# Transposing two chunks of P on TensorE: threshold attention with a maxout FFN on one Trainium2 core

## The chip, the cores and the metric

The kernel runs on one core of one Trainium2 chip (trn2). The metric is the device time of one execution in microseconds (us); lower is better. A core has five engines that run side by side, each with its own instructions in order: TensorE (PE, matmul; its weight loads are shown as PEld), VectorE (DVE), ScalarE (ACT), GpSimd (POOL) and SyncE (SP), which issues transfers here. PE writes into PSUM; DVE and ACT read it from there.

## The reference

Inputs are q, k, v of shape (8, 8, 576, 64) (batch, heads, rows, head size), a scalar tau of 0.02, three FFN weights w1, w2, w3 of (512, 768) and w_out of (768, 512). All are float32.

```python
scores = scale * np.matmul(q, k.transpose(0, 1, 3, 2))        # scale = 1/8
thresh = np.max(scores, axis=-1, keepdims=True) - tau
scores = np.where(scores >= thresh, scores, -1000000000.0)
scores = scores - np.max(scores, axis=-1, keepdims=True)
attn = np.exp(scores)
attn = attn / (np.sum(attn, axis=-1, keepdims=True) + 1e-09)
attn_out = np.matmul(attn, v)
x = attn_out.transpose(0, 2, 1, 3).reshape(B * S, H * D)      # 4608 x 512
h = np.maximum(np.maximum(x @ w1, x @ w2), x @ w3)
out = h @ w_out
```

## The kernel before

**Tiling.** The heads are taken in 16 groups of four (two groups to a batch). A group's scores are computed in nine chunks of 128 rows, each in two halves of 128 x 576, so there are 144 chunks and 288 halves. The variable `n` of a chunk is its place in this count, from 0. After both groups of a batch have their attention products, the batch's FFN runs: 18 hidden pieces (6 column blocks by 3 weights) and output pieces.

**An order written out by hand.** All engines are fed from one string, `ORDER`. Each letter issues one step, and the digit behind S, T, O and F names which of four PSUM slots (two banks each) it uses. `line` holds, for each letter, the queue of items whose earlier step has been issued. The engines run their own steps in the order of the string, and each step waits for its data and its buffers. What moves in the string moves on the engine. The letters that matter here:

- S: a half's score matmuls on PE (`scores`); T: PE transposes of q or k; O: a product of P and v on PE (`product`); F and B: the first and second half of an FFN piece on PE.
- m: DVE reads a score half and takes its maximum (`maximum`). e: ACT's first pass (`exponents`). n: ACT's second pass, or k: DVE's product with a mask (`numerators`).
- r: DVE's reciprocal of the sums. p: POOL scales one half into `P` in bf16 (`normalized`); a chunk takes two.
- t: SP issues a DMA transpose of `P` into `ptq` (`turned`). ptq is what the products read, one for each group.
- l, g, o: SP's loads of q, k, v, its loads of weights, its stores. y, z: POOL's casts of v and of weights; q: POOL's swapped copy of q.
- a, c: ACT's and DVE's copies of transposed q and k out of PSUM. x, w: ACT's and DVE's copies of a product. h, v: ACT's copy of a first FFN piece, and DVE's maximum. u: ACT's copy of an output piece.

**Masks.** `MASKED` has one digit for each of the 288 halves. With 1 the half is masked by DVE: m writes `z` into SBUF and so frees the PSUM slot, e is one ACT pass on that, and k is a DVE pass. With 0, m only reads, e reads PSUM and frees the slot, and n is a second ACT pass. So a 1 moves work from ACT to DVE.

**Buffers.** P has 6 buffers (`PBUFS`), `z` has 4 for each of the two halves (`ZBUFS`), ptq has 2.

Every step is recorded by a helper at one line, L90, so the profile names that line for nearly all of them; they are told apart by the tile names (sc scores, tp transposes of q and k, o products, ph hidden pieces, po output pieces, ptq transposed P).

Of the kernel before, what the change touches and what calls it, by code (L numbers as in the profile page):

```python
# [12 lines left out]
BF16 = mybir.dt.bfloat16  # L13
# [25 lines left out]
ORDER = """
lllS0llmlS1yelgS2ymylS3emgnlT0mleS1lakS2nlqermS3ylmeS0pmeS1kpS3elmS2nlzmelrmnT1pS0tcnperkT1pameS1zmteS3knpS0  # L40
rnmpemS2permeqS1mnqT3meqktepS0ncS2ntrpmS3npretprmeS1pmnS0tpmS3npmS1etpmeS0rT2mnplkeT1akgeS2qmgepmteS3rkpeknt
S0perrnmT2pncS3ptamepS1meqtrS2meyqnS3lmqeS0pmelpknT1lpS2nmeymeS3lrkepS0tcnT2rpnmS1tpnmaprrmS0eS2pmteS1pmT3ep
ctepmeT3O0ykntnyS2etrykpnO1wnprmaS0xptrS3meS2zmeS1mzgeS0mlnS3pmleS1pmelO2qmelpkteO0nrnklpS3nlwgxprrmS2leS0pm
eF3qtmT1eBqcF0eqkthBpnS2vS1nF3pmnF0pmBerBkepS2vhT1tnprmS0S3apmetS1zmeS2rmpeF3tmF0epBkepF1tnBvBznvS2ghS3rymnF
0gmS1eplBrkepF2tnmF3BnpvBnqvT1S0hprrcT2S3pamS1eymzF2emBeqgkF0etyS3nS1vpnmtF2pBmezBveS3prgnS0mtS1phrmT3epO2me
tzeF0wpnS1gcqS2nmBqnmO3zekepgS1xvlF2nS3mtnF0rrmpBeBlpveS1lphS2mntF3zmeBrpS0evS1lpnmF2lnpS3rmleBptmS1nzvS0nS3
mtpnS2rpeF1rmepmtepS0mBepmtekF3ektekT2uBarklpukS0uqlS2urS1mlnS3pmleO0pmlepmelO2wtnkS1xrS0tepmF2myF3eBkepT1tB
hcF0nqvT2T1laByrcynS3qvS2nlqmF1tnpF0meS3pBelmBlhrrF2kpelS1vnBlprF3mnlS0pveBtprmS1hS2pmeS3tpmeS0pmF2emF1eBkeT
3BvatF0nvqT2T3BkqlaS1nrcS3phmtS2npmF0epF1mteBqkBeqF3lnvS2lnBrvplS0hmtpS1F3meS2mteBrmepS0vnpO1rekpnO3mtnpweS2
yrrtxS1mF0yymT3epBcnS1pvS2nptF3meS0pmeBomT2hS1okeF0omF3ntBkaBervS1ponrF2vpemS0ptuS3mpeF2metknT1T3rknBparrceS  # L50
0puS3mqtuS1mpeS2mpeS3lmF0peomepS1ketqT3S2ncBqnmlqnmlO3ekluktO1urnwperrS0pxS3mptnS2mS1pempS3etmF0peF2meBlkBel
S1khoF3nrmlF0pnBtvpBerrvS2phlS1mnpS3tmF0peS2mpeBmeF3vF1eoBkntS0vnBS2rmhpS3mepS1mteyF2mF0eyBkteBnrvT3pF1aovT2
ynBplrcS3hplS0mnyF2lmF1elBykepBlnvT3tS0aS2vnO3rrmtpnmpeS1weptS2mS0prmO3eqtmeqF1eqlT0S2xqcBnlpmS3hlpS0meF2ymF
1elBknlF3vnBokBetS2hvS0nrrF3mpF1mpeBkBpetF2vnprS0uvnT3ptmS2aS1pmeS0trmF3epmnpkeS2tS0ermpBnmopnkS1uS2rurompS0
eF3ompelmpeS2lkpeS0lmS1elqBmelqmetkO2unktO0erwpurkpT1txT2cS3apF0nmtT1qS2ceBqmnS1yF3hmF2eyrBpeBvptnF0pS1vnBrm
tpS3hS2pmeS0mtS1eF3meF2meBkBeF0knF1vnBBrvhpS3nvT0pF2akyF1tnBmyS0velByrmlS3phS2rlempF1lmyeF0pklBepS3tnvS2nBrm
ptO1meprvepS2wnS3plmF0nF1rmepBlkeqS2lBhmtT3nyS0vnS2mqlO1emtpecT2xT0rS3pacF1eqmF2lnyBklqeT0BvlaS3khoS1qnmF0tF
2pmeBrBopnvS3teprvF0pnrmS1puS2meS3prmS0epF1tmepmepT2ktBeqncT3tuS0kaS2urqmS3tnpmS1nF0pmemteS3repS1mS2lepmBely
kteS3kuO1rumplnmlpO0ewterpT2xS1cqnoS3mpF0nF2metBkeBkF1hlF3nvBlnrrS0pvlnBpmS2lhS1ymleF0mtS3epBmepF2vF1etkBnS0
vnS3rmBnpS2rhmpF0emF1pteBkpBerF3vnS2ptvnT0pBramS1pthS0mepF3meqtT2rBecpS1nvylT0ynS2pmlS3amlS1eomS0elO2rmpeome  # L60
plO3ketnwT1F0nctF2xkBnBrvpS1hrF3pmS0qBemqS2onvF1yeF0mBopkeF3tyBnS2vqhBrlrnmpT1S0vaptS2empF1S3mpelBkeplF0vntS
2rumS1pnS0mtepF3rmepmetqS2kS0epBnmmteS1rkepS2lmuS0ulpmS1nlymT3yetF2cekeT3oBrknpamoS0npS3mnS1qtmuO0qurrmqelO2
wpelkpelS0xS3meptF2mS1peBemytF0hrkT3pBecF2nS1vpnS3rymtBpnmS0epS1vlnF3mF2etBmeBkhF0lkeF3nBrvpS1nrvBpnS2mptS0h
mpeS3meF2tmF1eBkeBlrvnT0plS3ravlpS2nlmqF0nlS1mqeBtrrmpF2eS3phBlmepS0tvepS1mS2npS3mepO0meknO1meownT3orxkT2pS0
tacF1nF2qrmeBtpS3evpBmS0tyhF1meT2yBcqoeF3rpkT2F0aptBnvBnS2pvS1hqtmF3nqT0meBrS1npvF2npmT3BactS1ervF3prmS0pueS
2ompF3ekqelmT1ntS0qcnBpmekteS2S1urrmpF0uompekS3eptS2nmS1pnmlO3ermtpekO2pnwS1ykxtyS3emS2BomeyrmepS1rukpS2uoF3
meF0opmnBtykBhpS1ervS2eptmO3pO0mxnS3txS2rmepF0empF1ekBtBevF3hkS2nS0mnBrmF1npF2vepBkBtS0hvO3emO2xkS1xerS3rpmF
2mpF0eF1kpteBnBvpF3BvtBrhkpF2S0vS1prmBptmF3eF0pveBtBhS1vS2mS3mF0F1mBkBF2vhF3keBeO0vnO1kF2kxeBwurS1rvpS0mpS2F
3mpetmpeS0eoF1mnketBknkBurrupoF2puF0hptF3uvF2pvF1hF0tvF3rvpF2hF1vopF0vF3thF2vF1vF0hoF3vF2ovF1hF0vF3vO2uoO1wF
0xF3F2hF1vF3vF2hF1vF3vF2hF1vF3vF2hF1vF3vF2hF1vF3vF2hF1vBvF3uuooBF2uuuooo  # L70
"""


# [28 lines left out]
def kernel(  # L102
# [485 lines left out]
    def flow(what, fn):  # L588
        while True:
# [13 lines left out]
    def issue(what, where):  # L603
        if what == "S":
            c, r = next(todo["S"])
            c[r] = scores(Ls[c["g"]], c["idx"], r, where)
            line["m"].append((c, r))
        elif what == "T":
            g, n, r = next(todo["T"])
            p = transposed(Ls[g], n, r)  # L610
            p.first(where)
            line["a" if n == "q" else "c"].append((p, g, r))
        elif what == "O":
            p = next(todo["O"])
            p.first(where)
            for k, fn in (("x", p.scalar), ("w", p.vector)):
                if fn:
                    line[k].append(fn)
        elif what == "F":
            p = next(todo["F"])  # L620
            p.first(where)
            if p.second:
                pending.append(p)
            else:
                line[p.kind].extend(p.done)
        elif what == "B":
            p = pending.pop(0)
            p.second()
            line[p.kind].extend(p.done)
        elif what == "m":  # L630
            c, r = line["m"].pop(0)
            c["bias", r] = maximum(c, r)
            line["e"].append((c, r))
        elif what == "e":
            c, r = line["e"].pop(0)
            exponents(c, r)
            line["k" if masked(c["g"], c["idx"], r) else "n"].append((c, r))
        elif what in "nk":
# [36 lines left out]
_INS = ['q', 'k', 'v', 'tau', 'moe_w1', 'moe_w2', 'moe_w3', 'moe_w_out']  # L675
# [31 lines left out]
```

## Time and profile before

| what | before |
|---|---|
| time, median of 3 runs | 446.44 us (446.01 to 447.31) |
| profiled execution, its own time | 447.21 us |
| its span from first to last instruction | 445.4 us |
| mean granted TensorE clock | 0.985 |
| busy PE, DVE, ACT, POOL | 425.5, 395.1, 393.8, 314.9 us |
| P transposes by DMA | 144, median 3.9 us from issue to landing |
| first product of P and v starts | 54.9 us |
| first FFN piece starts | 67.8 us |

Times within the execution are counted from the start of the span. An engine's busy time counts its instructions' spans; spans of neighbouring instructions on an engine overlap, so the start-to-start time is shorter than a duration. The page's slices cut the span into 40 parts of about 11 us, with the busy share in tenths.

### The profile page before, as it was taken

What the parts mean: (1) busy time and instruction counts of PE and PEld (TensorE: products, weight loads), DVE (VectorE), ACT (ScalarE), POOL (GpSimd) and SP (SyncE); (2) the same over time, 40 slices, a digit from 0 to 9 for tenths busy, and PEclk for the clock granted to TensorE, in tenths of its full rate; (3) what the DMA queues carried; (4) which work ended last, traced back from release to release, by engine and by line L of the source; (5) the groups of instructions that cost most, each with busy time, mean ns of one, the idle gap of its engine ahead of it and who ended that gap; (6) DMA issues with size and microseconds to landing.
All of it is one profiled execution on the core that took longest, in us unless ns stands there. A gap on an engine that the chain in (4) does not pass through costs nothing.

```text
span 445.4 us, 14085 instructions
## 1 busy us (share of the span) xinstructions
PE 425.5 (96%) x5195; PEld 316.4 (71%) x5195; DVE 395.1 (89%) x1093; ACT 393.8 (88%) x801; POOL 314.9 (71%) x417
## 2 busy tenths in 40 slices
PE   7677799999999999999999999999999999999995
PEld 5455557767787767778687767867687778777772
DVE  4889999999999999989989998999999999989641
ACT  4999999999999999999998999999999999956422
POOL 3797999989686686686768884859767789562300
PEclk9967999999999999999999999999999999999999
DMA  7999999999999988999996999899998978872902
GB/s 235 344 163 216 251 169 241 227 245 230 222 250 195 244 165 177 252 191 253 187 175 158 238 206 167 207 249 203 208 208 192 249 121 172 149 122 34 217 13 107
DMA packets 212773, 87.44 MB, mean 196 GB/s; under 512 B 185824, under 2 KB 199648, under 8 KB 212704
## 3 DMA queue, kind: packets, MB, share of 16 engines
q1 hardware_dynamic: 212000, 85.69, 92.2%
q8 instruction: 41, 0.67, 0.6%
q10 hardware_dynamic: 704, 0.85, 0.6%
q14 instruction: 28, 0.23, 0.2%
HBM read 34.60 MB, written 9.44 MB: 99 GB/s over the span
## 4 chain that ended last, share of the span: by engine, by line
PE 82%; DVE 6%; ACT 5%; issue 3%; DMA 2%; POOL 1%; SPq 1%; DVEq 0%; POOLq 0%; ACTq 0%
PE ph L90 30%; PE sc L90 28%; PE po L90 11%; PE o L90 9%; ACT z L90 4%; PE tp L90 4%; DVE unused L90 2%; DVE z L90 2%; DMA km<-in_k_dram 1%; DMA qm<-in_q_dram 1%; POOL P L90 1%; SPq L90 1%; DVE hm L90 0%; DVE hT L90 0%; DVE kt L90 0%
## 5 line engine op out<-in xcount | busy, mean ns | idle before, releaser
L90 POOL TENSOR_SCALAR P<-z,rs 128x576 bf16<-128x576 f32 x288 | 229.5, 812 | 85.1 <-DVE rs L90 36.8
L90 PE MATMUL sc<-kt,qs 64*128 64x256 f32 (+2 forms) x640 | 180.5, 423 | 4.8 <-DVE z L90 1.7
L90 PE MATMUL sc<-kt,qt 64*128 64x320 f32 (+2 forms) x640 | 181.1, 434 | 4.1 <-ACT z L90 4.1
L90 PE MATMUL ph<-xt,w 64*128 64x288 bf16 (+2 forms) x2160 | 163.8, 283 | 0.3
L90 PEld LDWEIGHTS <-w 64*128 64x128 bf16 (+1 forms) x2160 | 124.8, 94 | 31.0 <-issue 5.1
L90 DVE TENSOR_SCALAR_CACHE_REDUCE unused<-sc 128x576 bf16<-128x576 f32 x183 | 133.3, 750 | 8.5 <-PE sc L90 7.5
L90 ACT ACTIVATE z<-sc,nm 128x576 f32<-128x576 f32 x183 | 131.2, 740 | 10.5 <-DVE unused L90 6.8
L90 ACT ACTIVATE z<-z 128x576 f32<-128x576 f32 x183 | 123.5, 681 | 0.1
L90 PEld LDWEIGHTS sc<-kt,qs 64*128 64x128 f32 (+1 forms) x640 | 94.3, 181 | 25.5 <-ACT z L90 7.0
L90 PEld LDWEIGHTS sc<-kt,qt 64*128 64x128 f32 (+1 forms) x640 | 94.5, 181 | 17.8 <-ACT z L90 9.2
L90 DVE SCALAR_TENSOR_TENSOR z<-z 128x576 f32<-128x576 f32 x105 | 85.2, 822 | 0.8 <-ACT z L90 0.8
L90 DVE TENSOR_SCALAR_CACHE_REDUCE z<-sc 128x576 f32<-128x576 f32 x105 | 77.7, 752 | 5.8 <-PE sc L90 3.5
L90 ACT ACTIVATE z<-z,nm 128x576 f32<-128x576 f32 x105 | 79.0, 773 | 3.5 <-DVE z L90 3.2
L90 POOL COPY qs<-qt 64x512 f32<-64x512 f32 (+1 forms) x63 | 44.6, 707 | 15.7 <-ACT qt L90 12.6
L90 PE MATMUL po<-wo,hT 64*128 64x512 bf16 (+1 forms) x480 | 54.0, 356 | 0.1
L90 ACT ACTIVATE hm<-ph 128x576 bf16<-128x576 f32 (+2 forms) x54 | 32.1, 594 | 18.5 <-PE ph L90 18.1
L90 DVE TENSOR_TENSOR hm<-ph,hm 128x576 bf16<-128x576 f32 (+2 forms) x54 | 37.0, 686 | 12.8 <-PE ph L90 11.6
L90 PEld LDWEIGHTS <-hT 64*128 64x128 bf16 (+1 forms) x480 | 29.6, 97 | 17.1 <-issue 2.9
L90 DVE TENSOR_TENSOR hT<-ph,hm 128x576 bf16<-128x576 f32 (+2 forms) x54 | 37.1, 688 | 3.3 <-PE ph L90 0.8
L90 PE MATMUL o<-ptq,vb 128*64 128x64 bf16 (+2 forms) x544 | 38.7, 282 | 0.0
L90 ACT ACTIVATION_READ_ACCUMULATOR z<-z 128x1 f32 x183 | 36.4, 199 | 0.0
L90 PEld LDWEIGHTS <-vb 128*64 128x64 bf16 x544 | 22.6, 111 | 15.1 <-issue 6.1
(33 smaller groups left out, 275.2 us busy)
## 6 DMA issues: line engine op xcount, KB each, us to landing
vm<-in_v_dram SPq DMA_DIRECT2D x32, 256.0 KB, 5.2
out_dram<-ob SPq DMA_DIRECT2D x31, 256.0 KB, 2.8
qm<-in_q_dram SPq DMA_DIRECT2D x15, 512.0 KB, 4.4
km<-in_k_dram SPq DMA_DIRECT2D x15, 512.0 KB, 5.1
stage<-in_moe_w_dram SPq DMA_DIRECT2D x9, 512.0 KB, 5.2
ptq<-P SPq DMA_TRANSPOSE x144, 3.9
stage<-in_moe_w_out_dram SPq DMA_DIRECT2D x3, 512.0 KB, 4.6
qm<-in_q_dram SPq DMA_DIRECT2D x16, 64.0 KB, 2.7
```

Source lines behind the costliest of these rows:

```text
L90: ins = fn(*a, **kw)
```

## The change

Chunks 7 and 9 (the eighth and the tenth) are not given to t but to a new step X. It runs nine PE transposes of 128 x 128 from P into a PSUM slot, read as bf16, and a new step i copies the 1152 columns from there into ptq on ACT. A bf16 identity is made on POOL at the start.

```diff
+TURNED = (7, 9)
...
+    identb = one.tile([128, 128], BF16, name="identb")
+    pool.tensor_copy(out=identb, in_=identf)
...
             if n:
-                line["t"].append(c)
+                line["X" if c["n"] in TURNED else "t"].append(c)
...
+    def turned_on_tensor(c, where):
+
+        L = Ls[c["g"]]
+        if "pt" not in L:
+            L["pt"] = pt_pool.tile([128, 9, W], BF16, name="ptq")
+        ps = bank("pp", where).bitcast(BF16)
+        for m in range(9):
+            tensor.transpose(ps[:, 128 * m:128 * m + 128], c["P"][:, 128 * m:128 * m + 128], identb)
+
+        def done():
+            scalar.activation(out=L["pt"][:, :, c["idx"] * 128:(c["idx"] + 1) * 128],
+                              in_=ps[:, 0:W].rearrange("p (m u) -> p m u", m=9), func=AF.Copy)
+        line["i"].append(done)
...
+        elif what == "X":
+            turned_on_tensor(line["X"].pop(0), where)
-        elif what in "hvuxw":
+        elif what in "hvuxwi":
             line[what].pop(0)()
```

`ORDER` and `MASKED` are new throughout. The number of every letter is the same but for t (142 instead of 144) and two each of X and i; 105 halves are masked in both. The masks differ in 44 of the 288 places. The first four lines of the order (before, then after; the line breaks are the source's) and the first line of the masks:

```diff
-001100101001000000011101001010000001100010001000101000011000100000100000
+100100100001000100011101001010001011000010001000101000011000100000100100
...
-lllS0llmlS1yelgS2ymylS3emgnlT0mleS1lakS2nlqermS3ylmeS0pmeS1kpS3elmS2nlzmelrmnT1pS0tcnperkT1pameS1zmteS3knpS0
-rnmpemS2permeqS1mnqT3meqktepS0ncS2ntrpmS3npretprmeS1pmnS0tpmS3npmS1etpmeS0rT2mnplkeT1akgeS2qmgepmteS3rkpeknt
-S0perrnmT2pncS3ptamepS1meqtrS2meyqnS3lmqeS0pmelpknT1lpS2nmeymeS3lrkepS0tcnT2rpnmS1tpnmaprrmS0eS2pmteS1pmT3ep
-ctepmeT3O0ykntnyS2etrykpnO1wnprmaS0xptrS3meS2zmeS1mzgeS0mlnS3pmleS1pmelO2qmelpkteO0nrnklpS3nlwgxprrmS2leS0pm
...
+llS0llS1mlyleS2mlyS3eymlkS0lemnlT1lmnS2greS3pmgepmleS0keT3lT2ramplaS1qnS2lmqelmnqS0tkeymeS1nrcS2pnrS3mqnmpT1
+empetS0rcpekS1epT2nmS3znmnmS1perrmpeS0petmpnS3keplerS1mpnlS0pnmlaptS3mezS1emtyeS2ymektS0eknS1rmtpX3kpermiS2p
+tkeS3qnT0mgnrpcT1nprmS0apemS1pemtT3eprmS2ekqteS0mnS1pgnlmqnlcqS0elmpX3erkpT2etkiS1pnmS3azrtrmS0nmpeS2rmpeS1p
+emtepO3mepkntO0ynknT2pewxS1rtrncS3pS0mpT2mpS1etmpaemS2zgetS3meqS0rmeS2qmgO1npkepnO3rmnptkepeS0wlxS2rmnplS1mF
```

In the string the first F comes after 51 S, 11 T and 4 O in both orders. The first X stands behind the 27th S, the second behind the 35th.

More of the change, by code (lines that the diff above doesn't have):

```diff
@@ L24 @@
 MASKED = """
-001100101001000000011101001010000001100010001000101000011000100000100000
-000011111001100001001001001001000001011100101001000110001010010000010011
-000010011101100001001100100001001010001100010111000001000100000110000101
-001001001101100000110001000100100100001100100011100111010011010111110110
+100100100001000100011101001010001011000010001000101000011000100000100100
+000011111001100001000001001001000001011100100001100110001010010001001001
+000110010110011001001100100001001010000110010110010001000100000110000101
+001001011101100000110001000100100100001001000111110011101000001100111010
 """
@@ L39 @@
 ORDER = """
-lllS0llmlS1yelgS2ymylS3emgnlT0mleS1lakS2nlqermS3ylmeS0pmeS1kpS3elmS2nlzmelrmnT1pS0tcnperkT1pameS1zmteS3knpS0
-rnmpemS2permeqS1mnqT3meqktepS0ncS2ntrpmS3npretprmeS1pmnS0tpmS3npmS1etpmeS0rT2mnplkeT1akgeS2qmgepmteS3rkpeknt
-S0perrnmT2pncS3ptamepS1meqtrS2meyqnS3lmqeS0pmelpknT1lpS2nmeymeS3lrkepS0tcnT2rpnmS1tpnmaprrmS0eS2pmteS1pmT3ep
-ctepmeT3O0ykntnyS2etrykpnO1wnprmaS0xptrS3meS2zmeS1mzgeS0mlnS3pmleS1pmelO2qmelpkteO0nrnklpS3nlwgxprrmS2leS0pm
-eF3qtmT1eBqcF0eqkthBpnS2vS1nF3pmnF0pmBerBkepS2vhT1tnprmS0S3apmetS1zmeS2rmpeF3tmF0epBkepF1tnBvBznvS2ghS3rymnF
@@ L45 @@
[L45 to L69, printed above, removed]
@@ L70 @@
-0xF3F2hF1vF3vF2hF1vF3vF2hF1vF3vF2hF1vF3vF2hF1vF3vF2hF1vBvF3uuooBF2uuuooo
+llS0llS1mlyleS2mlyS3eymlkS0lemnlT1lmnS2greS3pmgepmleS0keT3lT2ramplaS1qnS2lmqelmnqS0tkeymeS1nrcS2pnrS3mqnmpT1
+empetS0rcpekS1epT2nmS3znmnmS1perrmpeS0petmpnS3keplerS1mpnlS0pnmlaptS3mezS1emtyeS2ymektS0eknS1rmtpX3kpermiS2p
+tkeS3qnT0mgnrpcT1nprmS0apemS1pemtT3eprmS2ekqteS0mnS1pgnlmqnlcqS0elmpX3erkpT2etkiS1pnmS3azrtrmS0nmpeS2rmpeS1p
+emtepO3mepkntO0ynknT2pewxS1rtrncS3pS0mpT2mpS1etmpaemS2zgetS3meqS0rmeS2qmgO1npkepnO3rmnptkepeS0wlxS2rmnplS1mF
@@ new lines @@
+3nplF0rmelqBlekT1zBlhcF2teS3vpnS1mF0gnpmBteqBrveS3prhS2mpS1nmS0pemzeS3mteT1F2pmaF0kyeBgF1keqBnvBtnyS3rvpS2hr
+mS0tpnF1mepBkepF3nmF2zBnvBnvT0zgS1hctT3yS2arrmS0etpmF3epmBerpS1tevS2pnmF0F3qgmeBtykeBpS1hrvS2pnS3mnzT0tmO1nc
+pngmO0pewlzekF1lxS2qelBrrmnS0qlvS3nylF2mpeF1lmpeBgkBpetS0vhS3pnrrS1mtF2pmeBpmeS0pvnF3zmeS2tBrempS1nvS0plS2em
+zS3nmS1pntrF0epmnpmtF2erkpemS3etBpmekeT1tkBuaktuS3rkupS1urS0mlnS2pmeO3rqmelmpetO1wpnkpS0xlS3emlF1prmF2elpBke
+lT0qBhtcF3nT1vT0aBlcnS2qlvS1nqlF0mntpS3meF2ymBetBrrhkpF1evS0nBymS3npvS2epmF1pS0metBmeS3rhS0pmteF2pmF1eBrkpet
@@ new lines @@
+BvnF3pT0nvT2BtarcT1phS0apS2mnS3tqmeF1qmF0eyBkoeyS2ovnBF3lrnmqS1lvBepS2lmhpF0meBtrepS3vS1nqmS2lnpmO0lerklnpO3
+lwnlprermtS0pxF1mepT3tBceyS2vpnS0mF3nyS1pmeBmF0etkF2hBekBtnvS1nF3rrmpS0vupeT1mS3ptaS2mepF1ketknT0T3nBrrompal
+rcqeS2ouS3pmluS0pmetF1mpekpeS2tnS3mS0pnmBermlpeT3S2eqcS0tuqkO3uqnomnO1pmewteS2rrkxS3pS0nmS1pmF2epmtF3empBeBk
+teS0khF1nrF2mlpBnvlpBerrlS3vphlS0mnyS1tmF2epS3melBpmeF1pvF0nBkeS2rvnBpS3mhyS1ymeS0lymeF3tmpF2eBkeBtvnF1rT0nv
+pBalkT3pS2hrcS0nF1ptrmnF3pmBepBlveT0S2qlraS1mqntO0mqevqelS2wpnS3lmF1nptS0mepBmelO2kelkthT3S0xrcpS1tmF2pS3mey
@@ new lines @@
+F0meBrBepvF1npF3vtnBkyS2hrS0tmpnF1rnmpBBeoprvS0npT2ovF3apomS1upteS2myS0emF3elymetkS1eS0nrmpS2tmBepmeklS0eS1k
+uF2ourkpnlmS3nlpBrmelpmelS0kyuS3lnrmqtO1empeO0twpekuqT1xS3cT2ptF0ramT1pnBcF2etqkS1hqBnmF3nS0prvBepmtF1S2yrve
+BmS3phS0metyS1ymS2epF3mepF0meBtkBeF1knF2lrnvBlpBhvplS3nvF1tnF0mT2kBalS3veBlmS2hlrS1rrepmoF0mpeF3kpBteBvnS2pn
+S1mytnO0mevyeF1plwS2nlprrBmoS3phoF0mpeS1tkpBeS2mnoS3mqeO1lvqelmylT0xpT2cT3laS1cnT0qlF2meqtF3keBBkaS1thrqrF0v
+nS3mpnF2mpBeBrrpveS1pnvF0onpmS3uS2qemS0tpmS1eS3mpeF2tmperknpT0tBmepncT1tukS3uS0rrempoF2mpepalS0eS3ytmS1nmBpe
@@ new lines @@
+tmeqkS0eqS3oumO1utrkpemO0npwekT2txS1ncS3F0mnlF2rrlkepBBmhF1pnvF0epBtrS2npvBnmpS3lhS1plmeF2lmS0eBlmeF3vlF1ekB
+tnS2rvnpS0ornBmyS3thmpF2empF1eBkpBevF0ntS3ryrvnyT2BarmS1tyhS2mpeF0mpelT3BpeclS1lnpvS2lnpmT3tS0apmS1emS3qelO2
+mqelmqnO0lweokeT2tkF1xF3nrrpBntBrcqS0nvF2phmS1pS3emBpmF0eptF1vepBknBtF2nvS3hrBrmptT0S1vpaS3meptF2mS0peBkeylF
+1mnqS3luvnS0trmS1peF2mepmetS3knS1rBmeplrkepoS0umS3umtqeS1mT2pnF0clnpmetT3S2keBkearrmpS1uS3kupS2nmO0eprtmepmO
+1ekqtewS3xS2prmnoF0pmS1eBkqeoF3mhtT2BprceS0vpnF2S1mpntBmpnS3vS0eylF1melF2meBlkBelF3khF0lnrvBplnS1rrvtpBnmS2p
@@ new lines @@
+hS3mpetS0mpF2emF1eyBkpetBvT3nS0ryavlS2nrqmF3nS1myleBrlmF2eptS0hpBmeS3pvteS1pmS2npS0mepO3memetO1wnknT0lxT2rrc
+S3pnF1mptaF0keBqS2evtBqmS3hF1pmeT0lBqceF2vpnF0orBknptBnvT3S1hryoS2amF0omqT3elBcqnS2lF1revpT3mBptaS0nvpS3emF1
+ytqmF2urpnkepT1S3ecS0ntmqBmpekS1peS3rumF0uptrmepnS2pS3tnmS1pemO2emonkO3etrrwpS1xkpS2emS3BpmtepmeF1koeF2kouBS
+3okhBurmS1pnoS0myntO3mO1pxrveS0tyxF3ymepS2reS1pmeBpmteF2pvS0eBmtF3hkS1eF2mnBkBeF0knF1vnBBvhO3kO0xrvpS2xnrS3m
+pF0mpF1teBpeBvS2thrrS3pmS0pmF1eF2mpteBpeBvF3ntS0vnF1mnBrBphS2epS3mtF0meF2kBeF3vBvBhF1nvF0kO2ukO3rwBpxS0vpS2m
@@ L71 @@
+S3tS1rmepF0mepmeF3tknkeBkrBrupupnF2ptF1rhF0pvF2vpF1thF0upvF2uvF1htF3vF0vF2hoF1vF3vF0hoF2vF1ovF3hoF0vO2oO1wvF
+3xF2uoF0F1hF3vF0vF1hF3vF0vF1hF3vF0vF1hF3vF0vF1hF3vF0vF1hF3vBvF0uuoBF1ouuuooo
 """
@@ L595 @@
                 O=products(), F=pieces())
-    line = {k: [] for k in "menkrptahvuxwcq"}
+    line = {k: [] for k in "menkrptahvuxwcqiX"}
     casts = iter([w[1] for w in wl])
@@ L669 @@
         what = text[x]
-        if what in "STOF":
+        if what in "STOFX":
             x += 1
-        issue(what, int(text[x]) if what in "STOF" else None)
+        issue(what, int(text[x]) if what in "STOFX" else None)
         x += 1
```

## The prediction

> **What bounds the kernel now.** I read the page's busy times and slices first, then busy time by stage, then the waits of the early stage, then the chain of waits, then single rows for prices.
>
> ```profile
> PE 425.5 (96%) x5195; PEld 316.4 (71%) x5195; DVE 395.1 (89%) x1093; ACT 393.8 (88%) x801; POOL 314.9 (71%) x417
> ...
> PE   7677799999999999999999999999999999999995
> ...
> ACT  4999999999999999999998999999999999956422
> ...
> PEclk9967999999999999999999999999999999999999
> DMA  7999999999999988999996999899998978872902
> ```
>
> TensorE (PE) is full in every slice (11 us each) from the seventh on, but only 6 to 7 tenths busy before. ScalarE (ACT) is full from the second slice. So there are two stages: up to about 68 us PE has only score tiles and transposes to do, and ACT and VectorE (DVE) pace it; after that FFN pieces fill PE and PE paces everything.
>
> To see how much PE time each order needs, I took from the trace the time from each PE step's start to the next step's start, by kind of step and of its follower, from 75 us on, and summed the medians over the order (score, score: 0.534 us; first half of an FFN piece, second half: 0.490; product, score: 1.356). The order of before sums to 407.9 us. The first score starts at 7.1, the last step at 440.1, and 5.3 us follow to the end: 7.1 + 407.9 + x + 5.3 = 445.4 gives x = 25.1 us that PE lost. By stretches of 20 us the loss is 6.3, 10.0, 6.4, 1.8, 0.75, and within 0.4 of nothing after 100 us. Everything that an edit can win on PE lies ahead of the first FFN piece, which starts at 67.8 us.
>
> Busy time in the stretches where the granted clock changes (columns: stretch and length, then PE, PEld, DVE, ACT, POOL busy, clock, DMA share, GB/s):
>
> ```profile
> 19.24:26.07 6.83, 4.09 (x38) 2.42 (x36) 6.74 (x21) 6.83 (x16) 6.71 (x8) 1.00 1.18 252
> 26.07:32.89 6.82, 6.20 (x25) 4.79 (x27) 5.77 (x17) 6.82 (x16) 6.68 (x10) 0.50 0.90 148
> 32.89:39.72 6.83, 4.52 (x55) 2.61 (x53) 6.75 (x22) 6.50 (x13) 4.34 (x5) 1.00 1.15 229
> 39.72:46.55 6.83, 6.13 (x38) 5.21 (x38) 5.94 (x16) 6.33 (x15) 6.53 (x11) 0.50 0.92 172
> 46.55:53.37 6.82, 4.99 (x48) 3.23 (x47) 6.31 (x22) 6.82 (x16) 6.66 (x9) 1.00 1.12 307
> ```
>
> ACT is idle for 0.8 us of these 34, so ACT's work up to the first FFN piece is the bound there. Two stretches ran at half clock, each behind one in which PE was busy for 4.09 or 4.52 us; behind 4.72 (12.41 to 19.24) and 4.99 the clock stayed full. In the slow stretches DVE lost 1.05 and 0.88 us, ACT none and 0.50. The transfer engines are full too, but the waits between 12 and 80 us (total, times, longest) show nobody waiting for a transposed P:
>
> ```profile
> PEld sc L90 <- ACT z L90: 12.0, 15, 2.0
> PE sc L90 <- ACT z L90: 5.7, 6, 1.5
> ...
> POOL P L90 <- DVE rs L90: 2.2, 3, 1.0
> ...
> ACT z L90 <- DVE unused L90: 1.4, 5, 0.3
> ```
>
> PE waits for ACT to read a score tile and free its PSUM slot. That is the wait that ends last here.
>
> **The change part by part.** *The two P transposes taken from the queue.* A transpose on SP is 1.36 us of issue, and 3.9 to landing:
>
> ```profile
> L90 SPq DMA_TRANSPOSE ptq<-P x144: 1247/1359/4044, 19.5 to 419.1; - x144
> ...
> DMA to landing us min/median/max: 3.2/3.9/7.8
> ```
>
> The two cost 2.54 and 1.31 us of issue here. The products that read ptq show 0.0 us of idle before them, and POOL in this stretch waits for no P buffer. I price the relief at 0; its bound is the 3.85 us that leave SP, of which none is on the path while those rows hold.
>
> *The transposes on PE.* 18 matmuls of 128 columns with a 128x128 bf16 weight load each. The nearest row is the late FFN piece with 128x128 loads and 256 columns, 4 matmuls in 0.436 us, 0.109 each; by columns alone half of that. So 0.49 to 0.98 us each step, and I take 0.98 because every matmul has its own load. PE has 25 us idle here, so this is off the path. The first X stands behind the score that started at 36.52; its P (chunk 7) was done at 33.1. The second stands behind the one at 47.91; its P was done at 40.7. Neither should wait; the next scores queue behind each. Its identity is one copy on POOL before 6.37 us, where POOL's first real work starts: 0, and well under a 0.7 us copy if that idle time were gone.
>
> The trace speaks on the clock here: before 5.8 us PE had run only transposes, first 14 warm ones in 3.25 us (0.23 each), then 5 in 0.77 (0.15 each), so transposes did raise the rate. The Trainium skill says otherwise (TensorE: Matmul & The Clock Gate, Part 4: PE-mode transpose: such a transpose takes about 275 ns in a kernel, and full clock does not engage for it). By that rule the estimate for the 18 is 4.95 us, still in PE's idle time, and the clock term below would be 0; I go by the row.
>
> *ACT's copies.* The rows for PSUM copies on ACT, 654 ns for 576 columns and 380 for 256, give 0.856 ns a column, so 1.15 us for 1152, and 1.01 from start to start (0.53 for a 576 copy back to back, 0.27 for 256). ACT is full there, so they count. Behind each copy on ACT wait the next exponentials; one ACT step of 0.67 stands between the first X and its copy, so ACT may also wait 0.3 for the transposes (two steps in the second). Half a chunk costs ACT, unmasked, 0.64 + 0.58 + 0.09 = 1.31 from start to start:
>
> ```profile
> 37.45 0.74 ACT L90 ACTIVATE z<-sc,nm 128x576 f32<-128x576 f32 x1 [0.32 <-DVE unused L90]
> 38.09 0.68 ACT L90 ACTIVATE z<-z 128x576 f32<-128x576 f32 x1
> 38.67 0.19 ACT L90 ACTIVATION_READ_ACCUMULATOR z<-z 128x1 f32 x1
> 38.76 0.73 ACT L90 ACTIVATE z<-sc,nm 128x576 f32<-128x576 f32 x1
> ```
>
> *Masks.* Masked, it costs ACT 0.67, and DVE 0.68 more (its product step, from start to start). The total stays 105, but the first batch has 14 instead of 12 and the last 17 instead of 20; the last one costs ACT 1.9 where its slices are at 2 to 6 tenths: 0, or up to 1.9 if its part before those slices binds. Counted up to the first FFN piece in each order, ACT loses one 0.64 and one 0.67 and gains two copies of 1.01: **+0.7 us**. DVE gains 0.6, POOL nothing (43 P and 4 weight casts in both), SP loses 4 loads and 1 transpose; PE has 51 scores, 11 transposes and 4 products in both, and the two X. So the first FFN piece comes 0.7 us later, with the same useful PE work done.
>
> *The order at the start.* The chain of waits begins with a load behind which PE stood:
>
> ```profile
> 7.33 4.08 DMA qm<-in_q_dram
> 11.42 0.14 issue
> 11.55 0.54 PE tp L90 x10
> ```
>
> PE stood 1.46 us there with scores queued behind. The new order puts a fifth score ahead of that transpose, and masks chunk 0's first half, which frees its slot after DVE's read. ACT's gaps between 8.8 and 18 us are 0.46, 0.29 and 0.33, 1.1 in all; I take half: **-0.6** (ends 0 and -1.1).
>
> *The order later.* By the same pair medians the new order without X sums to 407.1, so 0.8 less (where a pair does not occur before, from the two kinds added); half of these differences are of single samples, so I take **-0.4** (ends -0.8 and +0.4).
>
> *The clock.* The first X adds about 1 us to the 4.52 us of the stretch before the second slow one, which puts it above 4.72. If the stretches fall alike, the second slow one goes, worth 0.5 (ACT) to 0.9 (DVE). They may fall otherwise, so: **-0.4** (ends 0 and -0.9).
>
> Where the stall goes: PE still waits for ACT at the end of the early stage, and after 68 us PE's own work is next. Sum: 0.7 - 0.6 - 0.4 - 0.4 = -0.7 on the profiled execution, span 445.4 to 444.7, or 447.2 to 446.5 with what lies around it. The median before is 446.44, 0.8 below that execution; so 445.7.
>
> **The rivals.** *Faster*: every order term at its far end and the slow stretch gone, 0.7 - 1.1 - 0.8 - 0.9 = -2.1, or 444.3; if both slow stretches go, another 1.0, 443.3. For it: PE's busy time of 4.52 lies only 0.2 below what kept the clock. Against: ACT, not PE, is full there.
>
> *Slower, by PSUM slots*: X takes one of four slots for 1.0 of transposes, up to 0.67 of ACT's running step and 1.15 of copy, 2.8 us in all, in the stage where PE's longest wait is for a slot. Three slots serve meanwhile; if ACT has no score in stock, it loses a quarter of that, 0.7 each. Then 0.7 + 1.4 with nothing won elsewhere is +2.1, 448.5. It decides once ACT idles over 0.7 us behind each X; against it, ACT's waits for scores in 12 to 80 us are 1.4 in all.
>
> *Slower, by the clock*: a lighter stretch at 12 to 19 us (4.72 now, 0.2 above the slow ones) gives a third slow stretch, 0.5 to 1.05, and 0.7 for ACT's work: +1.7, 448.1. The re-ordered FFN stage may also add waits of some tenths that the pair sums can't show.
>
> **How the numbers follow.** A measurement of this kernel tells about 0.3% (1.3 us) from no change. Forecast, about the same: 0.38. Faster: 0.36. Slots: 0.16. Clock or new waits: 0.10. The range reaches past the faster case's 443.3 and the slots' 448.5 by a little: 443.2 to 448.7. So faster 0.36, same 0.38, slower 0.26.
>
> **What would show it.** Right: first FFN piece at 67 to 68 us; PE's loss from 100 us on near nothing; ACT full from 20 to 70 us; two ACT copies of about 1.15 us from ptq's transposes; X without a wait for P. Wrong: PE's loss ahead of the first FFN piece changing by over 1.5 us; ACT idle behind an X; the first FFN piece at the same place and the loss later; or a wait for ptq that shows the queue mattered.

## The result and the profile after

The changed kernel takes 450.97 us (median of 4 runs, 450.43 to 451.66) against 446.23 for the kernel before (4 runs, 445.67 to 447.31). The ratio is 1.0104, 95% interval 1.0078 to 1.013: slower by 4.7 us, where 445.7 and a range up to 448.7 were forecast.

The profiled execution is one of the four: 450.43 us, span 448.6, mean clock 0.988. Its span is 3.2 us longer than that of the profiled execution before. The page of after, with the busy times, PE's and ACT's slices, the clock and the transfers (the helper's line is L91 in this kernel):

```profile
span 448.6 us, 14114 instructions
PE 426.7 (95%) x5213; PEld 317.5 (71%) x5213; DVE 396.2 (88%) x1093; ACT 396.1 (88%) x803; POOL 312.5 (70%) x418
PE   7787789989999999999999999999999999999995
ACT  4999999989999999999989999998999999985422
PEclk9987999999999999999999999999999999999999
DMA  8999999999999999999879998999999978855712
```

The early slices are much as before. New is an 8 in PE's ninth slice (90 to 101 us) and one in ACT's, in the stage where PE should be full. Busy time by stretches of 20 us (columns as in the prediction: PE, PEld, DVE, ACT, POOL, clock, DMA share, GB/s), first of after, then of before:

```profile
60.00:80.00 20.00, 18.84 (x239) 13.55 (x238) 19.25 (x53) 20.00 (x41) 18.49 (x23) 1.00 1.15 227
80.00:100.00 20.00, 18.14 (x238) 13.24 (x236) 18.98 (x46) 17.24 (x38) 17.73 (x23) 1.00 1.01 219
100.00:120.00 20.00, 19.94 (x218) 13.42 (x217) 19.28 (x59) 19.48 (x41) 14.91 (x20) 1.00 1.03 212
```

```profile
80.00:100.00 20.00, 19.86 (x260) 14.07 (x258) 18.98 (x51) 19.32 (x43) 18.52 (x24) 1.00 0.99 238
```

From 80 to 100 us PE is busy 1.7 us less than before and ACT 2.1 less, at full clock. DVE is busy for the same 18.98 us, but with 46 instructions instead of 51: some of them became longer. The waits of after between 85 and 102 us name the place, and the timeline of 88 to 99 us shows it (start, duration, engine, instruction; in brackets idle time before it and what ended that):

```profile
PEld tp L91 <- DVE hT L91: 2.0, 1, 2.0
PE tp L91 <- DVE hT L91: 1.4, 1, 1.4
```

```profile
90.71 1.46 POOL L91 TENSOR_SCALAR P<-z,rs 128x576 bf16<-128x576 f32 x2
...
90.96 2.81 DVE L91 SCALAR_TENSOR_TENSOR z<-z 128x576 f32<-128x576 f32 x1
...
92.12 1.03 POOL L91 CAST w<-stage 128x1024 bf16<-128x1024 f32 x1
...
93.96 0.74 DVE L91 TENSOR_TENSOR hT<-ph,hm 128x576 bf16<-128x576 f32 x1
...
94.75 0.46 PE L91 MATMUL tp<-identf,km 64*128 64x64 f32 x8 [1.45 <-DVE hT L91]
```

A masking product on DVE (a `k` of the order) took 2.81 us; the median of the 105 is 0.75, the next longest 1.28 (the longest in the kernel before: 1.66). It stands beside two P and a weight cast on POOL and ends 0.6 us after the cast. Behind it on DVE waits hT, the maximum that frees a PSUM slot, and for that slot wait PE's transposes of k.

By the prediction's account (each PE step's start to the next step's start, less the pair medians of before) the difference of the two profiled executions splits as follows, in us:

| | before | after |
|---|---|---|
| first FFN piece starts | 67.82 | 68.03 |
| PE's work from there on, by pair medians | 371.3 | 370.7 |
| PE's loss from there on | 1.03 | 4.43 |
| of it at 80 to 120 us | 0.82 | 3.12 |
| of it beyond 120 us | -0.36 | 0.88 |
| from the last PE step to the end | 5.27 | 5.43 |

0.2 - 0.6 + 3.4 + 0.2 makes the 3.2. Only the first 0.2 lies ahead of the first FFN piece.

### The profile page after: what moved, and what is told of

Same layout as the page of the kernel before. It is cut to its first block, busy times and chain, and to the rows that moved or that the text cites. A ratio compares the mean times of both kernels' runs of the same rounds, so it can differ in the third digit from the quotient of the medians.

```text
span 448.6 us, 14114 instructions
## 1 busy us (share of the span) xinstructions
PE 426.7 (95%) x5213; PEld 317.5 (71%) x5213; DVE 396.2 (88%) x1093; ACT 396.1 (88%) x803; POOL 312.5 (70%) x418
## 4 chain that ended last, share of the span: by engine, by line
PE 78%; ACT 8%; POOL 4%; DVE 4%; issue 3%; DMA 1%; DVEq 0%; POOLq 0%; SPq 0%
PE ph L91 30%; PE sc L91 28%; PE po L91 9%; PE o L91 8%; ACT z L91 7%; PE tp L91 3%; POOL P L91 3%; DVE z L91 3%; DVE unused L91 1%; DMA qm<-in_q_dram 1%; POOL w L91 1%; DMA out_dram<-ob 1%; ACT ob L91 0%; ACT qt L91 0%; DVE hT L91 0%
## 5 line engine op out<-in xcount | busy, mean ns | idle before, releaser
L91 POOL TENSOR_SCALAR P<-z,rs 128x576 bf16<-128x576 f32 x288 | 225.2, 796 | 91.0 <-DVE rs L91 31.7
L91 PE MATMUL sc<-kt,qt 64*128 64x320 f32 (+2 forms) x640 | 181.1, 431 | 5.7 <-ACT z L91 4.2
L91 PE MATMUL sc<-kt,qs 64*128 64x256 f32 (+2 forms) x640 | 179.9, 420 | 5.3 <-ACT z L91 2.4
L91 PE MATMUL ph<-xt,w 64*128 64x288 bf16 (+2 forms) x2160 | 165.8, 283 | 0.3
L91 PEld LDWEIGHTS <-w 64*128 64x128 bf16 (+1 forms) x2160 | 127.0, 94 | 30.7 <-issue 5.9
L91 DVE TENSOR_SCALAR_CACHE_REDUCE unused<-sc 128x576 bf16<-128x576 f32 x183 | 133.6, 750 | 7.0 <-PE sc L91 6.2
L91 ACT ACTIVATE z<-sc,nm 128x576 f32<-128x576 f32 x183 | 131.4, 741 | 7.2 <-DVE unused L91 3.2
L91 ACT ACTIVATE z<-z 128x576 f32<-128x576 f32 x183 | 123.7, 683 | 0.0
L91 PEld LDWEIGHTS sc<-kt,qs 64*128 64x128 f32 (+1 forms) x640 | 92.6, 178 | 26.5 <-ACT z L91 10.0
L91 PEld LDWEIGHTS sc<-kt,qt 64*128 64x128 f32 (+1 forms) x640 | 92.9, 179 | 19.9 <-ACT z L91 7.8
L91 DVE TENSOR_SCALAR_CACHE_REDUCE z<-sc 128x576 f32<-128x576 f32 x105 | 78.0, 752 | 11.4 <-PE sc L91 9.2
L91 ACT ACTIVATE z<-z,nm 128x576 f32<-128x576 f32 x105 | 79.1, 775 | 7.9 <-DVE z L91 7.5
L91 DVE SCALAR_TENSOR_TENSOR z<-z 128x576 f32<-128x576 f32 x105 | 85.3, 828 | 0.1
L91 POOL COPY qs<-qt 64x512 f32<-64x512 f32 (+1 forms) x63 | 46.1, 731 | 14.6 <-ACT qt L91 10.2
L91 PE MATMUL po<-wo,hT 64*128 64x512 bf16 (+1 forms) x480 | 53.7, 356 | 0.1
L91 DVE TENSOR_TENSOR hm<-ph,hm 128x576 bf16<-128x576 f32 (+2 forms) x54 | 37.0, 686 | 10.2 <-PE ph L91 9.3
L91 ACT ACTIVATE hm<-ph 128x576 bf16<-128x576 f32 (+2 forms) x54 | 32.1, 595 | 14.3 <-PE ph L91 13.9
L91 PEld LDWEIGHTS <-hT 64*128 64x128 bf16 (+1 forms) x480 | 29.2, 97 | 18.0 <-issue 4.0
L91 DVE TENSOR_TENSOR hT<-ph,hm 128x576 bf16<-128x576 f32 (+2 forms) x54 | 37.1, 687 | 3.8 <-PE ph L91 1.7
L91 PE MATMUL o<-ptq,vb 128*64 128x512 bf16 (+2 forms) x544 | 38.7, 281 | 1.7 <-DMA ptq<-P 1.3
L91 ACT ACTIVATION_READ_ACCUMULATOR z<-z 128x1 f32 x183 | 36.7, 201 | 0.0
L91 PEld LDWEIGHTS <-vb 128*64 128x64 bf16 x544 | 23.0, 111 | 16.2 <-issue 7.4
```

The source lines that it names most:

```text
L91: ins = fn(*a, **kw)
```

## The experiments

Each ratio is against the kernel before on the same chip, with its 95% interval; 1.001 is 0.45 us. The losses are those of the table above, from each kernel's one profiled execution.

### X alone, and the new order alone

**e1_x_old_order** has the order and masks of before, with X and its copies put in by hand:

```diff
-mgepmteS3rkp ... mT2pncS3ptamepS1m ... epS0tcnT2rpnm
+mgepmeS3rkp ... mT2pncX1S3paimepS1m ... epS0tcX1niT2rpnm
```

> The order and masks of before, with X and its copy for chunks 7 and 9 put in by hand behind the second T's copy (slot 1), and the two t taken out. Theory 'order' (the newly fitted order and masks cost the 4.7 us, X itself is nearly free): within 1.5 us of before, 446 to 448. Theory 'X' (the slot, ACT's copies of 1.12 us each, two more steps on full engines): most of the 4.7, 449 to 451, with ACT idle or PE waiting for a slot behind each X.

Measured: 1.0066 (1.0042 to 1.009). The first FFN piece starts at 70.77, 3 us later than before, and the loss after it is 0.79, as before. At 449.99 us this is what theory 'X' said: put into the old order by hand, X does cost time.

**e2_new_order_no_x** has the order and masks of after, and all chunks transposed by DMA:

```diff
-TURNED = (7, 9)
+TURNED = ()
-S1rmtpX3kpermiS2ptke ... mS1pemtT3epr ... S0elmpX3erkpT2etkiS1pnmS3
+S1rmtptkpermS2ptke ... mS1pemttT3epr ... S0elmperkpT2etkS1pnmS3
```

> The new order and masks, with both chunks transposed by DMA again (t where X stood, and t for chunk 9 ahead of chunk 10's). Theory 'order': still 449 to 452. Theory 'X': back to 446 to 447.5. If the DMA relief is worth something in this order, it is slower than the changed kernel by up to the 3.9 us of SP issue.

Measured: 1.009 (1.0066 to 1.0114), 450.80 us as theory 'order' said, first FFN piece at 67.43, loss after it 5.10. **e3_after_again** is the changed kernel once more:

> The changed kernel again, for a second profile. Its first shows a DVE product step of 2.81 us at 91 us (others 0.74) beside POOL's P, P and weight cast, and PE waiting 1.45 us behind it. If that is set by the order, the long step and a PE loss of 2 to 3 us between 80 and 100 us come again; if it is chance, PE's loss there falls to under 1.2 us and the time is spread over other places or gone. Time 450 to 452.

Measured: 1.0106 (1.0083 to 1.0129), first FFN piece at 67.43, loss after it 4.49, with the same product of 2.80 us at 90.37. So in the new order X makes no difference that can be told, and the order with its masks alone brings the slowdown. Order and masks were changed together in every run, so which of the two it is stays open. The row of e2 for the stretch that was short of PE:

```profile
80.00:100.00 20.00, 17.95 (x239) 13.22 (x237) 19.31 (x46) 17.15 (x37) 18.03 (x24) 1.00 1.04 234
```

### What X costs in the old order

**f3_slot_only** runs X beside the DMA transposes and lets ACT read only 16 columns of its slot. **f4_copy_only** has two ACT copies of 1024 columns of P and no X:

```diff
 f3 (X1 and i as in e1, every t kept)
-            scalar.activation(out=L["pt"][:, :, c["idx"] * 128:(c["idx"] + 1) * 128],
-                              in_=ps[:, 0:W].rearrange("p (m u) -> p m u", m=9), func=AF.Copy)
+            scalar.activation(out=scr, in_=ps[:, W - 16:W], func=AF.Copy)
 f4 (i as in e1, no X, every t kept)
+                    line["i"].append(lambda P=c["P"]: scalar.activation(out=..., in_=P[:, 0:1024], func=AF.Copy))
```

> Before, with the two X (9 transposes each, at the places of the first experiment) added beside the DMA transposes; ACT reads only 16 of the 1152 columns, into a scratch tile. It prices the slot and PE's time without the copy. The first experiment cost 3.2 us. Theory 'ACT's copies' (2 x 1.0 on a full engine): 446.5 to 447.5. Theory 'slots' (one of four slots gone for a turn, PE behind it): 448 to 449.5.

> Before, with two ACT copies of 1024 columns of P into a scratch tile at the places of the first experiment's copies, no X on PE, DMA transposes kept. It prices ACT's time alone, 2 x 0.9 by the row. Theory 'ACT's copies': 448 to 449. Theory 'slots': 446.5 to 447.5.

Measured: f3 1.0029 (1.0011 to 1.0046), f4 1.0058 (1.0037 to 1.0079). Two copies of 1.13 us each on ACT cost 2.6 us (f4). f3 costs 1.3 us, at 448.93 what theory 'slots' said, but its rows name ACT once more: it waits 1.2 us for the transposes and takes 0.18 for each short copy, and nobody else waits. The sum, 3.9, is a little more than e1's 3.0, within the intervals. The rows of the tile pp, first in e1, then in f3, then in after:

```profile
L91 ACT ACTIVATE ptq<-pp x2: 1131/1131/1131, 42.1 to 51.7; 128x1152 bf16<-128x1152 bf16 x2
its engine sat idle before it (us, times) until:
  PE pp L91: 1.2, 2
```

```profile
L91 ACT ACTIVATE scr<-pp x2: 183/183/183, 43.3 to 52.4; 128x16 bf16<-128x16 bf16 x2
its engine sat idle before it (us, times) until:
  PE pp L91: 1.2, 2
...
who waited for it (us, times):
  ACT scr L91: 1.2, 2
```

```profile
L91 PE MATMUL pp<-identb,P x18: 219/219/229, 34.6 to 47.6; 128*128 128x128 bf16 x18
L91 ACT ACTIVATE ptq<-pp x2: 1122/1123/1124, 37.0 to 48.5; 128x1152 bf16<-128x1152 bf16 x2
its engine sat idle before it (us, times) until:
who waited for it (us, times):
  PEld sc L91: 0.8, 1
  POOL P L91: 0.6, 1
  PE sc L91: 0.6, 2
```

In e1 and f3 ACT waited 1.2 us for the transposes. In after ACT does not wait for them, and they wait for nothing: the new order places the copies better. What waits there are scores on PE, 0.6 us for the slot, where PE has time, and POOL, 0.6 us once.

### Which part of the order

**e4_new_then_old** takes the new order as far as the 20th F (about 107 us) and then the old one; **f2_old_then_new** the other way round:

```diff
 e4: ...emS3etBpmekeT1tk (after) | uBarklpukS0uqlS2... (before)
 f2: ...BepmtekF3ektekT2 (before) | BuaktuS3rkupS1ur... (after)
```

> The new order and masks (with X) up to the 20th FFN piece and the 83rd score half, about 107 us, then the order and masks of before. Theory 'early' (the loss sits ahead of 100 us, in the stall at 91 us): 449 to 451. Theory 'late' (many small waits in the newly fitted FFN stage): 446 to 448.

> The order and masks of before up to the 83rd score half (about 107 us), then the new ones; no X. Theory 'the newly fitted FFN stage costs about 1.2 by many small waits': 447.5 to 448.5, with PE's loss from 120 us on near +0.5 to +1 where before has -0.7. Theory 'all of the loss is early': 446 to 447.

Measured: e4 1.0096 (1.0074 to 1.0119), with 2.86 lost at 80 to 100, 1.34 at 100 to 120 and -0.74 beyond. f2 1.0062 (1.0038 to 1.0086), with 0.86 at 80 to 100, 1.47 at 100 to 120 and 1.19 beyond. The joined masks come to 107 halves in e4 and 103 in f2, instead of 105. At 451.06 us e4 is what theory 'early' said; f2, at 449.82, is slower than either of its theories. Both joints cost something: there PE waits for an output piece's copy on ACT, as the waits of f2 between 105 and 120 us show:

```profile
PEld sc L90 <- ACT ob L90: 1.7, 1, 1.7
PE sc L90 <- ACT ob L90: 1.2, 1, 1.2
```

What is lost at 80 to 100 us goes with the early part of the order, what is lost beyond 120 us with the late part. The times cannot divide it further: around the joint 1.3 to 1.5 us are lost, where after loses 0.3, and that is as much as what is sought.

### The long product

Theory: DVE's product is held while POOL works through P, P and the cast. Four kernels touch one letter each:

```diff
 f1_v_first: v ahead of k on DVE
-meBtykeBpS1hrvS2pnS3m
+meBtyvkeBpS1hrS2pnS3m
 g1_cast_later: the weight cast z behind the next two p
-pnS3mnzT0tmO1n ... ngmO0pewlze
+pnS3mnT0tmO1n ... ngmO0pzewlze
 g2_k_earlier: k ahead of the two m before it
-evS2pnmF0F3qgmeBtykeBpS1h
+evS2pnkmF0F3qgmeBtyeBpS1h
 g3_cast_twice: this one weight cast is issued twice
```

> The changed kernel with one DVE step moved: the maximum hT (v) that frees the slot for which PE waited at 94 us stands ahead of the masked product k that took 2.8 us in every profile of the new order. Theory 'DVE held by POOL': PE's loss of 1.65 us at 94 us goes, PE's loss between 80 and 100 falls from 2.4-2.8 to about 1, and the time falls by 1 to 1.7 us, to 449.5 to 450.5. Rival 'elsewhere': DVE is late by the same 2 us and PE loses it a little later; 451 to 452.

> The changed kernel with POOL's weight cast at 92.1 us moved behind its next two P. The long DVE product there ran from the second of two P to the end of that cast. Theory 'DVE's product waits until POOL pauses': it ends with POOL's second P and shortens from 2.8 to about 1.9 us; PE's loss of 1.7 at 94 us falls by 0.9, and the time by 0.5 to 1.2. Rival 'the product is long for another reason (its own data, a semaphore)': still 2.8, time 451 to 452.

> The changed kernel with that DVE product moved ahead of the two maxima before it, so that it starts before POOL's run of a copy, a cast, two P and a weight cast. Theory 'POOL's run': the product takes 0.75 to 1.3 us, POOL's next instruction is the one that is longer, PE's loss at 94 us is under 0.4, time 449 to 450.3. Rival: the stall moves with the product; 451 to 452.

> The changed kernel with the weight cast at 92.1 us done twice in a row (the same result). Theory 'POOL's run': the DVE product beside it grows from 2.8 to about 3.8 us, PE's loss at 94 us from 1.7 to about 2.7, and the time by 0.7 to 1.2. Rival: the product stays at 2.8 and the time within 0.5.

Measured, with the product's duration and the losses:

| | ratio (interval) | product | loss 80-100 | 100-120 | 120-140 |
|---|---|---|---|---|---|
| after | 1.0104 (1.0078 to 1.013) | 2.81 | 2.80 | 0.32 | 0.24 |
| f1 | 1.0073 (1.0054 to 1.0092) | 1.81 | 1.79 | 0.56 | 0.24 |
| g1 | 1.0072 (1.0051 to 1.0093) | 1.86 | 1.90 | 0.35 | 2.03 |
| g2 | 1.0069 (1.005 to 1.0089) | 0.75 | 1.01 | 0.73 | 1.61 |
| g3 | 1.0089 (1.0072 to 1.0107) | 2.84 | 2.41 | 0.73 | 0.25 |

The timeline of g2 and then of g3:

```profile
89.36 0.75 DVE L91 SCALAR_TENSOR_TENSOR z<-z 128x576 f32<-128x576 f32 x1
89.44 1.24 POOL L91 COPY qs<-qt 64x640 f32<-64x640 f32 x1
```

```profile
90.40 2.84 DVE L91 SCALAR_TENSOR_TENSOR z<-z 128x576 f32<-128x576 f32 x1
91.59 2.55 POOL L91 CAST w<-stage 128x1024 bf16<-128x1024 f32 x2
```

With the cast moved away the product takes one cast less (1.86). In after, f1 and g1 alike it ends 0.6 us behind the last of the instructions that POOL runs back to back beside it: the cast, and in g1 the second P. With the product moved ahead of POOL's run it takes 0.75, and it is POOL's copy that lengthens, to 1.24 from the 0.71 it takes in after. So the two hold each other up, and that POOL's run is what makes this product long is shown. That the product waits until POOL pauses, the form in which g3 was to prove it, is not; g3 speaks against it: a second cast did not lengthen the product. It ended 0.6 us into the second cast, which itself took 1.5 us instead of 1.03.

f1 moved the wait: hT is done early, and it is now a product of P and v that waits for z. The waits of f1 at 85 to 102 us:

```profile
PE o L91 <- DVE z L91: 1.3, 1, 1.3
```

The ratios of f1, g1 and g2 lie 0.3% under after's, but their intervals overlap with its interval, and in f1 the loss at 80 to 100 us falls to 1.79 where about 1 was expected. So the wait is explained; what it is worth in time is likely some 1.5 us, and not shown. In g1 and g2 what was won came back as a new wait at 124 to 126 us. The timeline of g2, and for comparison the same instruction of after:

```profile
123.86 0.52 PE L91 MATMUL tp<-identf,km 64*128 64x64 f32 x10 [1.18 <-DMA km<-in_k_dram]
```

```profile
123.83 0.49 PE L91 MATMUL tp<-identf,km 64*128 64x64 f32 x10
```

SP issued this load at 117.96 in after and at 117.56 in g2. A load takes about 6 us to land here, so in after the transposes reach it just in time, and PE gains nothing by coming sooner.

### The load as well, and the closing test

**h1_k_and_load_earlier** is g2 with the two loads moved ahead in the order, **h2_load_earlier** the changed kernel with the loads alone, **h3_early_fixed_then_old** is h1 as far as e4's joint and then the old order:

```diff
 h1 and h2
-nmS1pntrF0ep ... S1urS0mlnS2pmeO3rqmelmpetO1
+nmS1pnlltrF0ep ... S1urS0mnS2pmeO3rqmempetO1
 h3: ...emS3etBpmekeT1tk (h1) | uBarkpukS0uq S2urS1mln... (before, less the two loads)
```

> The changed kernel with the k that makes the long VectorE product at 91 us moved ahead of the two m before it (as in g2), and the two loads of group 5 that g2 issued at 117.6 us moved ahead in the order, behind the 32nd t instead of the 36th. Theory (two limits of the early FFN stage, one behind the other: the product held beside POOL, then the late load): the wait of TensorE at 94 us stays gone, the wait of 1.2 us for km at 124 us goes too, TensorE loses 0.5 or less there; the loss after the first FFN piece falls from 4.8 (g2) to 3.5 or less, ratio to the kernel before about 1.005. Rival (TensorE's loss is fixed by the amount of work that DVE, ACT and POOL have in this stretch, and a wait removed comes back elsewhere): the loss after the first FFN piece stays at 4.4 or more, ratio about 1.007 to 1.009.

> The changed kernel with only these two loads moved ahead. Theory: the product at 91 us still takes 2.8 us and TensorE still waits at 94, so the loss after the first FFN piece stays at 4.2 to 4.6 and the time is that of the changed kernel (ratio about 1.010). Rival (the late load is already part of the changed kernel's loss): half a microsecond or more comes off, ratio 1.008 or less.

> As h1 up to the 20th F and the 83rd score (about 107 us), then the order and masks of the kernel before, with one k put in at the joint. Theory (what is lost later comes from the later order, what is lost early from the two limits): beyond 120 us TensorE loses no more than in the kernel before (about 0.1 at 120 to 160, below nothing after), the loss after the first FFN piece is 1.0 to 2.5 with what the joint costs, ratio 1.000 to 1.004. Rival: a wait comes back in the early stretch and the ratio stays at 1.007 or more.

| | ratio (interval) | first F | loss 80-100 | 100-120 | 120-140 | beyond 120, all | after first F |
|---|---|---|---|---|---|---|---|
| h1 | 1.0081 (1.0056 to 1.0105) | 67.64 | 1.02 | 1.38 | 0.25 | 0.98 | 4.14 |
| h2 | 1.0091 (1.0055 to 1.0128) | 68.15 | 2.83 | 0.75 | 0.25 | 0.94 | 4.94 |
| h3 | 1.0056 (1.0033 to 1.0079) | 68.74 | 1.39 | 1.82 | 0.01 | -0.67 | 2.92 |

h2 is nearer to its theory, with the ratio near 1.009 and the long wait still there, so nothing shows that the load cost anything yet; its loss of 4.94 is above the 4.2 to 4.6 expected. In h1 both long waits are gone, at 94 and at 124 us, but its loss falls only to 4.14, between the theory's 3.5 and the rival's 4.4, and its time is that of g2. At 80 to 120 us it still loses 2.4 where before lost 0.8, now in small waits: part of the rival holds. h3, at 1.0056 and 2.92 lost, lies above its theory (1.004 and 2.5) and below its rival: its early part loses 3.2 with the joint, and beyond 120 us it loses as little as before. With f2 and e4 that settles where the late part of the loss sits: every kernel with the new late order loses 0.9 to 1.5 there (g1 and g2, with their wait at 124, apart), every one with the old one -0.3 to -0.7.

**g4_before_again**, the kernel before once more, shows how far such accounts repeat:

> The kernel before, for a second profile: 446 to 448. PE's loss from the first FFN piece on is a property of the order and comes again within 0.3 of 1.0 us; the start of the first FFN piece may move by 1 to 2 us with the stretches of half clock (67.8 in the first profile).

Measured: 0.9999 (0.9986 to 1.0012); first FFN piece at 67.81, loss after it 1.13.

No kernel here is faster than the kernel before.

## Why the prediction was wrong

**Order later (-0.4, ends -0.8 and +0.4): the step that failed.** The pair medians were right for what they can show: PE's work from the first FFN piece on falls by 0.6. But they price an order in which no step waits, and the new one waits. PE's loss from the first FFN piece on rose by 3.4 us: 2.3 at 80 to 120 us and 1.2 beyond, with 0.1 less before 80. The last bound of the sum, +0.4, should have held this; the price was put on PE's own steps alone, although 100 to 440 us of DVE, ACT and POOL work had been re-ordered too. The rival by new waits said so in one sentence, but priced them at some tenths and gave them, together with the clock, a chance of 0.10.

One part has a cause that runs confirm, the DVE product held beside POOL: with the product moved ahead (g2) PE loses 1.7 us at 80 to 120 us instead of 3.1, where the kernel before loses 0.8. The rest is small waits, and their cause is open. In h1, without that product's delay and without the late load, 2.4 us remain at 80 to 120 us. Beyond 120 us the profile names many waits of 0.2 to 0.4 us. PE's weight loads waiting for nothing that the profile shows are the largest group, 16.4 us in after against 15.2 before from 125 us on; but h3 has 16.4 too and loses nothing there, so they are not the cause.

The Trainium skill has a rule that bears on the long product (SBUF — State Buffer, SBUF: two separate sides): VectorE work with two SBUF inputs and GpSimd work that reads SBUF hold their shared ports for a whole instruction, and the other one blocks. The trace agrees in kind, by the 1.24 and 0.71 us of POOL's copy above. It differs in amount: whoever starts first has the ports, so by that rule the product should have come in behind the P that ran when it started, for an estimated 1.2 us in all, and the next longest take no more than 1.28. This one ended 0.6 us behind two P and a cast.

**Start (-0.6) and masks, ACT copies (+0.7).** The forecast of 67 to 68 us for the first FFN piece was just missed, 68.03, and the other runs lie about it: 67.0 to 68.7 in the other kernels with after's early order, g1's 69.31 apart. The old order gave 67.8, 67.8 and, in f2, 66.1. No gain at the start can be told from that spread, and no loss. On ACT itself the start's gain is seen: between 8.78 and 18 us ACT idles 1.15 us before and 0.35 in after (1.59 in g4, 0.69 in e3). With the +0.7 that nearly cancels, as the sum had it; that the first FFN piece stayed where it was is no proof of either term by itself. The copy's duration was right: 1.15 said, 1.12 measured.

**X on PE (0.98 each, off the path).** It waited for no P, as said. The size was the lower bound and not the one taken: the 18 transposes take 0.22 us each in duration, but follow one another by 0.056, so an X is 0.45 us from its first to its last start, and the next step started 0.15 behind that where it had nothing to wait for: 0.6 instead of 0.98. (e1's first X, in a half-rate stretch, went at 0.107.) By the figure of the Trainium skill that the prediction weighed (TensorE: Matmul & The Clock Gate, Part 4: PE-mode transpose: about 275 ns each) the 18 would be an estimated 4.95 us; the trace has 219 ns as a duration and 56 ns as the cost, and the trace decides. Off the path holds in the new order (e2 against e3). The slots rival is not borne out: in the old order X does cost 3.0 us (e1) and 1.3 without its long copies (f3), but f3's row shows ACT waiting for the transposes, and nobody waiting for the slot.

**Queue relief (0).** Right as far as the runs can tell, about 1 us: e2, which gives both transposes back to the queue, is no slower than e3. In after PE's first product does wait 1.3 us, put down to a transfer of P, one of the signs set for a wrong forecast. In e3, the same kernel, the same wait of 1.4 us is put down to ACT reading a score, and in both ACT's read of a score ends 0.05 us before the product starts. The waits of after between 12 and 80 us, then of e3:

```profile
PEld sc L91 <- ACT z L91: 13.2, 17, 2.0
PE sc L91 <- ACT z L91: 6.6, 10, 1.8
...
PE o L91 <- DMA ptq<-P: 1.3, 1, 1.3
```

```profile
PE o L91 <- ACT z L91: 1.4, 1, 1.4
```

It lies at 52 to 54 us, where PE has time, and does not show that the queue mattered; PE's great waits there are still for ACT to read a score.

**Clock (-0.4, ends 0 and -0.9).** The slow stretch did not go. The changed kernel has two half-rate stretches in its profiled execution, 3.4 us from 28.2 and 6.8 from 38.5, and none in e3's ahead of the last 2 us, so the change does not decide it: the kernel before has two as well, elsewhere in g4 than in the first profile. The mechanism failed too. The prediction took PE's busy time in the 6.83 us before as what decides, with a limit between 4.52 and 4.72. After lost the full clock behind 4.72 us, and behind 4.44 us in the stretch that holds the first X, which therefore did not make it fuller; e3 kept the full clock behind 4.17 us. The rows of after, then of e3:

```profile
21.41:28.24 6.83, 4.72 (x40) 2.57 (x42) 6.37 (x19) 6.83 (x16) 6.83 (x9) 1.00 1.29 126
31.65:38.48 6.83, 4.44 (x43) 2.72 (x43) 6.74 (x21) 6.25 (x11) 4.68 (x8) 1.00 1.24 187
```

```profile
12.49:19.32 6.83, 4.17 (x49) 2.19 (x48) 6.01 (x19) 6.83 (x15) 4.81 (x7) 1.00 0.98 292
```

What a half-rate stretch costs is open: e3, with 10.2 us less of it than after, starts its first FFN piece 0.6 us earlier; g4, with 6.8 us less than the first profile of before, starts it at the same place (67.81 and 67.82).

**The profile and the median.** The spans of the changed kernel's four runs are 448.6 to 449.8, and the profiled one is the lowest; of e3's six the profiled one is again the lowest, 448.1 against a median of 449.9. The kernel before has a median span of 445.2 in 23 runs, 445.4 in its profile. So about 1 us of the slowdown is in executions that were not profiled, and what it is made of is open.

One reading in the prediction was wrong, without weight in the sum: PE's sixth slice before is already at 9 tenths, so PE is short of work up to about 56 us and not up to the seventh slice.

The sign "the first FFN piece at the same place and the loss later" is the one that came.

## What to carry to other kernels

When an order written by hand is fitted anew, sum what each engine does and then look at what stands beside what: a sum over one engine's steps cannot show a wait, and 44 masks and most letters moved are a risk of their own, to be priced by the waits that the same stage has already shown. Take away the operation that a change is named after, and run its new order alone, before explaining the time by the operation. A wait that is removed is only worth the distance to the next limit, here a load that had been just in time.

## What the runs showed of the hardware

One DVE product of 576 columns took 2.81 us (2.80, 3.02 and 2.84 in e3, e2 and g3) instead of 0.75, beside back-to-back work on POOL; moved ahead of that work it took 0.75 and POOL's copy 1.24 instead of 0.71. Why this one passed over two changes of instruction on POOL, where the 104 others of the same kernel lose at most 0.5 us, no run shows. A PE transpose of 128 x 128 in bf16 with its own weight load took 0.056 us from start to start at full clock and 0.107 at half. Half-rate stretches are not a property of the program alone: ahead of the last 3 us the changed kernel had 10.2 us of them in one profiled execution and none in the other, the kernel before 13.7 and 6.8. An ACT copy of 1152 bf16 columns out of PSUM took 1.12 to 1.13 us.
